# FNet and gMLP on one core: third buffer for h2's rows, and waiting steps moved behind the splits that PE needs

## The chip, the core and the metric

The kernel runs on 1 core of one Trainium2 chip. The metric is the time of one execution on the device in microseconds (us): 943.65, the median of 3 runs (942.11 to 944.61). Only the order of the work and one buffer are changed, so a result is a difference of two such times.

## The reference

All tensors are float32. x is 2048 x 512, and c gives six rows (sa, ca, ga, sb, cb, gb) by a product with w_mod.

```python
h = _layernorm(x) * (1 + ca) + sa
a = h @ dft_hid_re.T;  b = h @ dft_hid_im.T
y = dft_seq_re @ a - dft_seq_im @ b          # 2048 x 2048 matrices
x = x + ga * y
h = _layernorm(x) * (1 + cb) + sb
z = gelu(h @ w_in)                           # 512 x 1792
z1, z2 = z[:, :896], layernorm(z[:, 896:])
x = x + gb * ((z1 * (w_sp @ z2 + b_sp)) @ w_out)   # w_sp 2048 x 2048
```

(The original writes these as einsums with a batch of 1; the equations are the same.)

## The kernel before

**Splits.** TensorE (PE) multiplies in fp32r. Every float32 operand is split into a high part (ScalarE, ACT: a copy into fp32r, line 604 for the pairs `ph`, 267 for `ah`) and a low part (VectorE, DVE: source minus high part, line 608 `pl`, 274 `al`). Each product is three matmuls (`matmul3`, lines 97 to 99): high by high, low by high, high by low. So PE needs, for each chunk of work, a `pl` or `al` that DVE has just made; each of these sits in a ring of three buffers (`ph`, `pl` and `al`; four for `ah`). Most chunks are twelve matmuls of 512 columns.

**Stages in order of time.** The *a* stage and three *t* stages make the sequence transform in four quarters t = 0 to 3. In a t stage there are 14 chunks of kind s and 16 of kind k. The k chunks use source blocks that are transposed on DVE (`tp`, line 539) straight out of a load buffer. The s chunks use sums and differences of blocks (one Strassen-like level): `f`, transposed at line 539, combined at 573 (`sum_f`). Results lie in PSUM banks `gs..c11`, `u`, `v`, `c22`; when a product form is done, banks are copied or subtracted (lines 682 and 688, t = 1 only, into `gs_u` and `um`), and at the end of a quarter `out_k` (line 723) adds `um` and stores to `g_d` through GpSimd's (POOL's) DMA queue. The *y* stage multiplies with the hidden-dimension matrices (`hr`, read as `hraw` and transposed at line 188), one block of 128 rows in 24 matmuls. For each row block m: `seed_y` (853) copies x into the PSUM bank `yp`, `split_g` (92, 93) makes `gh`/`gl`, PE accumulates, `post_y` (865) copies `x2` out and takes statistics (DVE 105, 107; POOL 109, 110, 117), `norm_y` (121) makes `h2` on ACT in a ring of two buffers, `post_h` (875 to 877) scales it on DVE and stores it to `h2_d` from POOL's queue. The *z1* stage multiplies `h2` (loaded again, transposed as `t`, line 238, or `hz`) with the first half of w_in, with seven product forms; banks `z1p`, `z1g`, the latter copied from the former at 988. Then *z2* (second half, banks `z2p`), the *w* stage with w_sp (`gw`), and the last product (`op`).

**Combinations of w_sp** are made on the way. For twelve of sixteen units in the z1 and z2 stages, four before: `load_s` reads three pieces (tile `sj`, lines 1056, 1058, SP's queue), `sum_s` adds and subtracts on DVE (1063, 1064, 1067) and stores to `s_d` (1070, POOL's queue). `sj` has two buffers in z1 and z2; in the t stages it uses the two buffers `stage`, which also hold the source blocks. A load into a buffer waits until the stores out of it have landed.

**What sets the order.** Nothing is scheduled by a tool: each engine runs its instructions in the order in which the program issues them. PE's chunks are numbered n, and `atd(n, f, ...)` puts a step f behind chunk n (n + 0.5: behind the low split that is made ahead there). `D1` = 32 is the first t chunk, `DT` = 30 chunks a quarter, `Y0` = 122 the first of 32 y chunks, `YE` = 154 the first z1 chunk. `CHUNKS[t]` is the order in which source blocks are loaded; a block's buffer is handed to the load two blocks on when its last transpose is issued (`block_done`). SP, ACT, DVE and POOL wait in order: whatever waits holds the rest of its queue.

Of the kernel before, what the change touches and what calls it, by code (L numbers as in the profile page):

```python
# [8 lines left out]
F32 = mybir.dt.float32  # L9
F32R = mybir.dt.float32r  # L10
AF = mybir.ActivationFunctionType
ALU = mybir.AluOpType

P = 128
# [5 lines left out]
def fnet_gmlp_kernel(  # L20
# [32 lines left out]
    nc = tc.nc  # L53
    S, D = x.shape[1:]
# [3 lines left out]
    NQ = S // Q  # L58
# [66 lines left out]
    def at(n, f, *a):  # L125
        fill.setdefault(n, []).append((f, a))
# [10 lines left out]
    def quad_s(t, role):  # L137
# [1 line left out]

    src = [quad((cr, ci)[j], 0, g) for g in range(NQ) for j in range(2)]  # L140
    CHUNKS = {1: (("k", 1, 0), ("k", 1, 1), ("s", 2, 21), ("s", 2, 11), ("k", 1, 2), ("k", 1, 3), ("s", 2, 22)),
              2: (("s", 3, 21), ("s", 3, 11), ("k", 2, 0), ("k", 2, 1), ("k", 2, 2), ("s", 3, 22), ("k", 2, 3)),
              3: (("k", 3, 0), ("k", 3, 1), ("k", 3, 2), ("k", 3, 3))}
    order_b = {}
    for t in range(1, NQ):
# [5 lines left out]
    N2 = 4 * len(src)  # L151
# [71 lines left out]
    def turn_two(n):  # L223

        if n >= NE:
            return
        b, k = divmod(n - SKIP if n >= N3 else n, 4)
        st = stage[b]
        t = blocks.tile([P, 2, Q], F32, tag="t", bufs=2, name=f"t{n}")
        T[n], T[n + 1] = t[:, 0, :], t[:, 1, :]  # L230
        if n >= N4:
            nc.vector.transpose(t.rearrange("p r (b i) -> p r b i", i=32), st[:, :, :, 16 * k:16 * k + 32])  # L232
        elif n >= N3:
            for m in range(2):
                nc.vector.transpose(T[n + m].rearrange("p (k a i) -> p a k i", k=4, i=32),
                                    st[:, :, 32 * (k + m):32 * (k + m) + 32].rearrange("p (a k) i -> p a k i", k=4))
        else:
            nc.vector.transpose(t.rearrange("p k (b i) -> p k b i", i=32),
                                st[:, :, 32 * k:32 * k + 64].rearrange("p b (k i) -> p k b i", k=2))
        if n == N2:  # L240
            RAW[0, 1] = RAW[0, 6] = t
        elif n == N2 + 2:
            RAW[0, 2] = RAW[0, 3] = t
        if k == 2:
            stage.pop(b)
            load(b + 2)

    RAW = {}

# [40 lines left out]
    fpool, yp, hrp = [], [], []  # L290
# [366 lines left out]
    def set_of(t, role):  # L657

        return {"c11": 0, "u": 2 if t == 3 else 4, "v": 4 if t == 3 else 2, "c22": 6}[role]

    def mm_s(t, i):
        p, m = ORD[i // 2], i % 2
        acc = {1: "c11", 2: "c11", 5: "v", 3: "v", 6: "u", 7: "u", 4: "u"}[p]
        fresh = p in (1, 5) and t > 1
        if m == 0 and fresh:
            for f in range(2):
                C[acc, f] = bank(set_of(t, acc) + f, f"gs{t}_{acc}_{f}")
        if t not in UM and p == 5:
            UM[t] = outs.tile([P, 4, D], F32, tag="um", bufs=1, name=f"um{t}")
        u = at_unit["s", t, i]  # L670
        ph, pl = PH.pop(u), PL.pop(u)
        for c_ in range(2):
            for f in range(2):
                matmul3(C[acc, f], *form_v(p, 2 * m + c_, f), ph[:, c_, :], pl[:, c_, :],
                        fresh and m == 0 and c_ == 0, m == 1 and c_ == 1, not fresh)
        if m == 0:
            return
        for f in range(2):
            if p == 1:
                C["u", f] = bank(set_of(t, "u") + f, f"gs{t}_u_{f}")  # L680
                if t == 1:
                    nc.vector.tensor_tensor(C["u", f], C["c11", f], UM[t][:, f, :], op=ALU.subtract)
                else:
                    nc.scalar.activation(C["u", f], C["c11", f], AF.Copy)
            elif p == 5:
                um = UM[t][:, 2 + f, :]
                if t == 1:
                    nc.vector.tensor_tensor(um, C["v", f], um, op=ALU.subtract)
                else:
                    nc.scalar.activation(um, C["v", f], AF.Copy)  # L690
            elif p == 6:
                nc.scalar.activation(UM[t][:, f, :], C["u", f], AF.Copy)
            elif p == 7:
                C["c22", f] = bank(set_of(t, "c22") + f, f"gs{t}_c22_{f}")
                nc.scalar.activation(C["c22", f], C["u", f], AF.Copy)
# [171 lines left out]
        NRM["y", m] = norm([X["2", m]], "y")  # L867

    def norm_y(m):
        LN["y", m] = yp[0].tile([P, D], F32, tag="h2", bufs=2, name=f"h2_{m}")  # L870
        apply(LN["y", m], X.pop(("2", m)), NRM.pop(("y", m)))

    def post_h(m):
# [422 lines left out]
    lo_one(2)  # L1296
    lo_h(1)

    n_now = [0]

    def atd(n, f, *a):

        at(("d", n) if n < YE else N2 + int(n - YE), f, *a)
# [44 lines left out]
    for t in range(1, NQ):  # L1348
        o = D1 + DT * (t - 1)
        d = 8 if t == 1 else 0  # L1350
        for m in range(2):
            atd(o + d + 0.5 + m, sum_f, t, 6, m)
            atd(o + d + 6 + m, sum_f, t, 3, m)
        for j in range(2):
            atd(o + ((22, 29) if t == 1 else (21, 29))[j], *((out_last, j) if t == NQ - 1 else (out_k, t, j)))
        if t < NQ - 1:
            atd(o + (11 if t == 1 else 3.5), load_sb, t + 1, 12)
            for role, n, m in (((21, 13, 14), (11, 15.5, 16.5), (12, 17.5, 18.5), (22, 24, 25)) if t == 1 else
                               ((21, 3, 5), (11, 7.5, 8.5), (12, 9.5, 10.5), (22, 21, 23))):
                atd(o + n, turn_s, t + 1, role, 0)  # L1360
                atd(o + m, turn_s, t + 1, role, 1)
            for p, n, m in (((5, 26, 26.5), (7, 27, 28)) if t == 1 else ((5, 24, 26), (7, 27, 28))):
                atd(o + n, sum_f, t + 1, p, 0)
                atd(o + m, sum_f, t + 1, p, 1)

# [13 lines left out]
            atd(n + k + 1, sum_column, j, k)  # L1379
    atd(83, scale_columns)  # L1380
    for j, l, ns, m, k, plus_one in ((2, 37, (40, 41, 42), 44, 6, False), (4, 51, (56, 57, 58), 60, 3, True),
                                     (3, 58.5, (63, 64, 65), 66, 7, False), (5, 77.5, (82, 83, 85), 87, 0, False)):
        atd(l, load_mod, j)
        atd(ns[0], sum_mod, j, [0, 1])
        atd(ns[1], sum_mod, j, [2, 3])
        atd(ns[2], split_mod, j)
        atd(m, spread_mod, j, k, plus_one)
    early = ((44.5, 53), (85.5, 89), (86.5, 91), (112.5, 115.5))
    early += tuple((YE + n, YE + m) for n, m in ((14, 17), (15, 19), (19, 27), (21, 28), (28, 31), (29, 33), (32, 35),
                                                 (34, 37), (36, 39), (38, 41), (39, 42), (41, 44)))  # L1390
    for (n, m), u in zip(early, [(r, g, b) for g in range(2) for b in range(4) for r in range(2)]):
        atd(n, load_s, *u)
        atd(m, sum_s, *u, True)
        atd(m + (m < YE + 23), sum_s, *u, False)
    atd(93, load, order_b["k", 3, 0])
    atd(96.5, load, order_b["k", 3, 1])
    hrs = ctx.enter_context(ExitStack())
    o = D1 + 2 * DT

# [5 lines left out]
        tf.close()  # L1405
        yp.append(p2.enter_context(pool("ypool", "right")))

    for n, *todo in ((-6, (load_ht, 0)), (-3, (turn_ht, 0, 0)), (-2, (turn_ht, 0, 1)), (-1, (turn_ht, 0, 2)), (0, (turn_ht, 0, 3)), (8, (scale_w0, 0)),
                     (9, (load_ht, 1), (weigh_ht, 0, 0), (weigh_ht, 0, 1)), (10, (weigh_ht, 0, 2), (weigh_ht, 0, 3), (load_w0, 0)),
                     (12, (fold_ht, 0, 0), (fold_ht, 0, 1)), (13, (fold_ht, 0, 2), (fold_ht, 0, 3)),  # L1410
                     (14, (open_hr,), (split_acc, 0), (turn_ht, 1, 0), (scale_w0, 1), (read_row, 2, hrp)),
# [48 lines left out]
    for n, *todo in ((0, (load_gelu,)), (2, (change_w,)), (4, (load_wi, 0, 2)), (7, (hi_w, 1)), (8, (lo_w, 1)), (9, (hi_w, 2)), (10, (lo_w, 2)), (11, (sum_w, 5)),  # L1460
                     (12, (sum_w, 6)), (13, (hi_w, 6)), (14, (lo_w, 6)), (15, (sum_w, 7), (load, N2 // 4)), (17, (sum_w, 4)),
                     (18, (hi_w, 7)), (19, (lo_w, 7), (turn_two, N2)), (20, (prep_hi, N2), (hi_w, 4)),
                     (21, (prep_lo, N2), (load, N2 // 4 + 1), (lo_w, 4)), (22, (prep_hi, N2 + 1)), (23, (prep_lo, N2 + 1)),
                     (26, (turn_z, 1)), (27, (sum_z, 0)), (28, (turn_two, N2 + 2), (prep_hi, N2 + 2)), (29, (prep_lo, N2 + 2)),
                     (30, (prep_hi, N2 + 3))):
        for f, *a in todo:
            atd(Y0 + n, f, *a)

# [4 lines left out]
    n = 0  # L1473
    for u, (kind, t, i) in enumerate(units):
        for m in range(1 if kind == "s" else 2):
            ahead = kind == "s" or m and u > 2
            if ahead:
                pipeline(u)
            if kind == "a":
                mm_a(n)  # L1480
            elif kind == "s":
                mm_s(t, i)
            else:
                mm_k(t, i, m)
            n_now[0] = n
            run(("d", n))
            if ahead:
                lo_unit(u + 2)
            run(("d", n + 0.5))
            n += 1  # L1490
# [141 lines left out]
```

## Time and profile before

| | |
|---|---|
| median of 3 runs | 943.65 us (942.11 to 944.61) |
| the profiled execution | 942.02 us, of which 940.3 us from the first instruction to the last |
| granted TensorE clock, mean | 0.998 |
| PE busy | 927.7 us (99%) |
| DVE busy | 746.6 us (79%) |
| ACT busy | 433.4 us (46%) |
| HBM | 135.01 MB read, 43.00 MB written |

A row of a timeline gives start, length, engine, line, operation, the tile written and the tiles read (their numbers left out), shapes, count, and in brackets the idle time before it and what ended it. A matmul's shown length (0.39) is longer than its distance to the next, since matmuls are pipelined. The waits list counts only gaps of over 150 ns.

### The profile page before, as it was taken

The numbers are of one execution on the slowest core, as the hardware profiler recorded it, in microseconds if no ns is written. First come the engines' busy times: TensorE is split into PE (matmuls) and PEld (weight loads), VectorE is DVE, ScalarE is ACT, GpSimd is POOL, SyncE is SP. The second block draws the span as 40 slices with busy tenths as digits, with TensorE's granted clock in tenths as the row PEclk, the third lists the DMA queues.
The fourth block names the chain that finished last, engine by engine and source line by source line (L and its number), as shares of the span: only waits on it lengthen the run. The fifth ranks groups of instructions, "written<-read, shape, count | busy, mean of one in ns | idle before, by whom it ended". The sixth has DMA issues, their size and how long they took to land.

```text
span 940.3 us, 12142 instructions
## 1 busy us (share of the span) xinstructions
PE 927.7 (99%) x4088; PEld 768.2 (82%) x4088; DVE 746.6 (79%) x1016; ACT 433.4 (46%) x686; POOL 158.6 (17%) x312
## 2 busy tenths in 40 slices
PE   9999999999999999999999999999999999999998
PEld 6788878888778888887878999888888888888886
DVE  7879789899788884778768667998789688885972
ACT  3585344354354353555765456553544444331221
POOL 1331001100110004544323444301000000000000
PEclk9999999999999999999999999999999999999999
DMA  9998949798685626795799876997569746743641
GB/s 203 217 210 187 224 98 235 182 171 192 173 232 105 180 83 195 227 267 166 212 328 273 242 236 213 262 259 207 124 151 261 201 111 157 185 112 113 198 160 57
DMA packets 269375, 178.83 MB, mean 190 GB/s; under 512 B 135168, under 2 KB 233728, under 8 KB 269184
## 3 DMA queue, kind: packets, MB, share of 16 engines
q1 hardware_dynamic: 253744, 133.99, 59.3%
q0 software_dynamic: 12576, 41.44, 11.7%
q10 hardware_dynamic: 2992, 2.62, 1.2%
q8 instruction: 32, 0.52, 0.2%
q14 instruction: 31, 0.25, 0.1%
HBM read 135.01 MB, written 43.00 MB: 189 GB/s over the span
## 4 chain that ended last, share of the span: by engine, by line
PE 71%; issue 11%; DVE 7%; DMA 5%; POOL 2%; SPq 1%; ACT 1%; DVEq 0%; ACTq 0%; POOLq 0%
PE gw L98 9%; PE gw L99 9%; PE gw L97 9%; PE op L99 3%; PE op L98 3%; PE op L97 3%; PE gp L98 2%; PE gp L99 2%; PE gp L97 2%; PE z2p L97 2%; PE z2p L99 2%; PE z2p L98 2%; PE gs_c L98 2%; PE gs_c L99 2%; PE gs_c L97 2%
## 5 line engine op out<-in xcount | busy, mean ns | idle before, releaser
L98 PE MATMUL gw<-al,bh 128*128 128x512 f32 x400 | 155.7, 389 | 0.1
L99 PE MATMUL gw<-ah,bl 128*128 128x512 f32 x400 | 155.6, 389 | 0.0
L97 PE MATMUL gw<-ah,bh 128*128 128x512 f32 x400 | 155.6, 389 | 0.0
L274 DVE TENSOR_TENSOR al<-t,ah 128x512 fp32r<-128x512 f32 x136 | 92.5, 686 | 61.9 <-PE gw L98 35.3
L267 ACT ACTIVATE ah<-t 128x512 fp32r<-128x512 f32 x136 | 84.9, 626 | 101.6 <-PE gw L99 56.0
L98 PEld LDWEIGHTS gw<-al,bh 128*128 128x128 f32 x400 | 75.1, 188 | 16.2 <-DVE al L274 0.5
L99 PEld LDWEIGHTS gw<-ah,bl 128*128 128x128 f32 x400 | 75.1, 188 | 15.5
L97 PEld LDWEIGHTS gw<-ah,bh 128*128 128x128 f32 x400 | 75.1, 188 | 15.5
L232 DVE STREAM_TRANSPOSE t<-stage 128x1024 f32<-128x1024 f32 x56 | 69.4, 1239 | 0.1
L604 ACT ACTIVATE ph<-f 128x1024 fp32r<-128x1024 f32 x42 | 44.4, 1058 | 40.4 <-PE gs_c L99 12.4
L1106 ACT ACTIVATE bh<-z 128x512 fp32r<-128x512 f32 (+1 forms) x56 | 32.8, 586 | 62.4 <-PE gw L98 60.6
L608 DVE TENSOR_TENSOR pl<-f,ph 128x1024 fp32r<-128x1024 f32 x42 | 50.7, 1214 | 11.6 <-ACT ph L604 11.5
L98 PE MATMUL gs_c<-pl,hh 128*128 128x512 f32 x144 | 56.3, 391 | 1.3 <-DVE pl L608 1.1
L99 PE MATMUL gs_c<-ph,hl 128*128 128x512 f32 x144 | 56.1, 389 | 0.0
L97 PE MATMUL gs_c<-ph,hh 128*128 128x512 f32 x144 | 56.1, 389 | 0.0
L604 ACT ACTIVATE ph<-tp 128x1024 fp32r<-128x1024 f32 x35 | 36.9, 1055 | 39.3 <-PE gs_v L99 15.9
L539 DVE STREAM_TRANSPOSE tp<-stage 128x1024 f32<-128x1024 f32 x36 | 44.4, 1232 | 4.4 <-DMA stage<-in_A_dft_seq_im_dram 4.1
L1070 POOL DMA_DIRECT2D s_d<-sj x48 | 26.6, 554 | 122.3 <-DVE sj L1063 105.0
L608 DVE TENSOR_TENSOR pl<-tp,ph 128x1024 fp32r<-128x1024 f32 x35 | 42.3, 1210 | 5.6 <-ACT ph L604 5.6
L98 PE MATMUL z2p<-wil,ah 128*128 128x448 f32 x128 | 46.7, 365 | 0.0
L97 PE MATMUL z2p<-wih,ah 128*128 128x448 f32 x128 | 46.7, 365 | 0.0
L99 PE MATMUL z2p<-wih,al 128*128 128x448 f32 x128 | 46.7, 365 | 0.0
(288 smaller groups left out, 2235.9 us busy)
## 6 DMA issues: line engine op xcount, KB each, us to landing
stage<-s_d SPq DMA_DIRECT2D x128, 128.0 KB, 2.9
stage<-in_A_dft_seq_re_dram SPq DMA_DIRECT2D x52, 256.0 KB, 6.6
s_d<-sj POOLq DMA_DIRECT2D x48, 256.0 KB, 5.2
stage<-in_B_w_sp_dram SPq DMA_DIRECT2D x96, 128.0 KB, 3.1
stage<-in_A_dft_seq_im_dram SPq DMA_DIRECT2D x44, 256.0 KB, 5.3
sj<-in_B_w_sp_dram SPq DMA_DIRECT2D x16, 512.0 KB, 6.7
stage<-h_d SPq DMA_DIRECT2D x32, 256.0 KB, 7.0
gr<-g_d SPq DMA_DIRECT2D x12, 512.0 KB, 5.7
```

The source lines that it names most:

```text
L97: nc.tensor.matmul(acc, ah, bh, start=first, stop=False, skip_group_check=go_on)
L98: nc.tensor.matmul(acc, ah, bl, start=False, stop=False, skip_group_check=go_on)
L99: nc.tensor.matmul(acc, al, bh, start=False, stop=last, skip_group_check=go_on)
L232: nc.vector.transpose(t.rearrange("p r (b i) -> p r b i", i=32), st[:, :, :, 16 * k:16 * k + 32])
L267: nc.scalar.activation(AH[n], source(n), AF.Copy)
L274: nc.vector.tensor_tensor(AL[n], source(n), AH[n].bitcast(F32), op=ALU.subtract)
L539: nc.vector.transpose(dst.rearrange("p k (b i) -> p k b i", i=32), st[:, :, 64 * m:64 * m + 64].rearrange("p b (k i) -> p k b i", k=2))
L604: nc.scalar.activation(pair_of(PH, u, "ph"), source_unit(u), AF.Copy)
L608: nc.vector.tensor_tensor(pair_of(PL, u, "pl"), source_unit(u), PH[u].bitcast(F32), op=ALU.subtract)
L1070: nc.gpsimd.dma_start(s_d[m, r, g][b * P:(b + 1) * P, :], a)
L1106: nc.scalar.activation(BH[p, k][:, :w], b_of(p, k), AF.Copy)
```

## The change

- `h2` gets three buffers in place of two.
- A new helper `later` puts a step half a chunk on, behind the low split made there. The subtractions of t = 1 (lines 682, 688) go through it. Some other steps get half a chunk more in the tables: `out_k` and `out_last`, first sums of w_sp units.
- In t = 2 the block ("k", 2, 3) is loaded ahead of ("s", 3, 22), and the turns and sums that need the latter come two or three chunks later.
- hr's real part is loaded 1.5 chunks earlier, and its four turns come 4.5 to 5.5 chunks later, spread. The split of `wm5` comes one chunk earlier. The first two blocks of t = 3 are loaded 2 and 1.5 chunks earlier.
- z1's second turn, `turn_two(N2 + 2)`, and its splits (`t130`, `ah130`, `ah131`, `al130`) come 4 to 5 chunks earlier, within y; the load that this turn used to issue keeps its place as a step of its own.
- From the first w_sp unit of z1 on, the twelve pairs (load, sum) get new places: the first two sums come 3 chunks later with the same loads, so six and seven chunks behind them.

```diff
-              2: (("s", 3, 21), ("s", 3, 11), ("k", 2, 0), ("k", 2, 1), ("k", 2, 2), ("s", 3, 22), ("k", 2, 3)),
+              2: (("s", 3, 21), ("s", 3, 11), ("k", 2, 0), ("k", 2, 1), ("k", 2, 2), ("k", 2, 3), ("s", 3, 22)),
...
         if k == 2:
             stage.pop(b)
-            load(b + 2)
+            if n != N2 + 2:
+                load(b + 2)
...
+    def later(f, *a):
+        at(("d", n_now[0] + 0.5), f, *a)
...
-                    nc.vector.tensor_tensor(C["u", f], C["c11", f], UM[t][:, f, :], op=ALU.subtract)
+                    later(nc.vector.tensor_tensor, C["u", f], C["c11", f], UM[t][:, f, :], ALU.subtract)
...
-        LN["y", m] = yp[0].tile([P, D], F32, tag="h2", bufs=2, name=f"h2_{m}")
+        LN["y", m] = yp[0].tile([P, D], F32, tag="h2", bufs=3, name=f"h2_{m}")
...
-            atd(o + d + 0.5 + m, sum_f, t, 6, m)
+            atd(o + (7.5 if t == 1 else 0.5) + m, sum_f, t, 6, m)
...
-    early += tuple((YE + n, YE + m) for n, m in ((14, 17), (15, 19), (19, 27), (21, 28), (28, 31), (29, 33), (32, 35),
-                                                 (34, 37), (36, 39), (38, 41), (39, 42), (41, 44)))
+    early += tuple((YE + n, YE + m) for n, m in ((14, 20), (15, 22), (22, 28), (24, 29), (29, 32), (30, 33), (32, 35),
+                                                 (33, 37), (35, 39), (37, 41), (39, 42), (41, 44)))
...
-    for n, *todo in ((-6, (load_ht, 0)), (-3, (turn_ht, 0, 0)), (-2, (turn_ht, 0, 1)), (-1, (turn_ht, 0, 2)), (0, (turn_ht, 0, 3)), (8, (scale_w0, 0)),
+    for n, *todo in ((-7.5, (load_ht, 0)), (1.5, (turn_ht, 0, 0)), (2.5, (turn_ht, 0, 1)), (4.5, (turn_ht, 0, 2)), (5.5, (turn_ht, 0, 3)), (8, (scale_w0, 0)),
```

The order of PE's instructions is the same. DVE around the last k chunks of t = 2, before (`pl57` and `pl58` are low splits that PE needs; `stage21` is the block that was loaded last, `f3_22` a block for t = 3):

```order
L608 TENSOR_TENSOR pl56_2118<-tp56_2057,ph56_2093 128x1024
L317 TENSOR_SCALAR wm5_2035<-wm5_2035,sc_136 128x512
L319 SCALAR_TENSOR_TENSOR wm5_2035<-wm5_2035,sc_136 128x512
L539 STREAM_TRANSPOSE tp58_2137<-stage21_2097 128x1024
L723 TENSOR_TENSOR um2_1727<-gs2_v_0_1725,um2_1727 128x512
L723 TENSOR_TENSOR um2_1727<-gs2_v_1_1726,um2_1727 128x512
L539 STREAM_TRANSPOSE f3_22_2161<-stage20_2015 128x1024
L348 TENSOR_SCALAR col1_141<-col1_141 128x4
L349 TENSOR_SCALAR col2_142<-col1_141 128x4
L319 SCALAR_TENSOR_TENSOR wm5_2035<-wm5_2035,sc_136 128x512 x2
L608 TENSOR_TENSOR pl57_2167<-tp57_2095,ph57_2135 128x1024
```

and now:

```order
L609 TENSOR_TENSOR pl56_2118<-tp56_2057,ph56_2093 128x1024
L318 TENSOR_SCALAR wm5_2035<-wm5_2035,sc_136 128x512
L320 SCALAR_TENSOR_TENSOR wm5_2035<-wm5_2035,sc_136 128x512
L540 STREAM_TRANSPOSE tp58_2137<-stage20_2015 128x1024
L349 TENSOR_SCALAR col1_141<-col1_141 128x4
L350 TENSOR_SCALAR col2_142<-col1_141 128x4
L320 SCALAR_TENSOR_TENSOR wm5_2035<-wm5_2035,sc_136 128x512 x2
L609 TENSOR_TENSOR pl57_2155<-tp57_2095,ph57_2135 128x1024
L729 TENSOR_TENSOR um2_1727<-gs2_v_0_1725,um2_1727 128x512
L729 TENSOR_TENSOR um2_1727<-gs2_v_1_1726,um2_1727 128x512
```

`um2` and the turn of `f3_22` moved from ahead of `pl57` to behind it, and `tp58` reads the block that is loaded first. On DVE in z1, before (`al148` to `al150` are low splits that PE needs, `sj002` the w_sp unit):

```order
L1063 TENSOR_TENSOR sj002_4169<-sj002_4169 128x512
L1064 TENSOR_TENSOR sj002_4169<-sj002_4169 128x512
L901 TENSOR_TENSOR wil1_0_4245<-wraw1_0_3995,wih1_4243 128x896
L274 TENSOR_TENSOR al148_4271<-hz3_4126,ah148_4237 128x512
L1067 TENSOR_TENSOR sj002_4169<-sj002_4169 128x512
```

and now:

```order
L907 TENSOR_TENSOR wil1_0_4241<-wraw1_0_3995,wih1_4239 128x896
L275 TENSOR_TENSOR al148_4267<-hz3_4126,ah148_4237 128x512
L907 TENSOR_TENSOR wil1_1_4272<-wraw1_0_3995,wih1_4239 128x896
L275 TENSOR_TENSOR al149_4286<-hz3_4126,ah149_4269 128x512
L944 TENSOR_TENSOR hz2_4024<-hz2_4024 128x1024
L275 TENSOR_TENSOR al150_4309<-hz3_4126,ah150_4288 128x512
L1069 TENSOR_TENSOR sj002_4169<-sj002_4169 128x512
L1070 TENSOR_TENSOR sj002_4169<-sj002_4169 128x512
L275 TENSOR_TENSOR al151_4327<-hz3_4126,ah151_4311 128x512
```

Three low splits now stand ahead of the first sum of `sj002`. On ACT late in y, before (`yp` rows are seeds, `x2` rows the copies out of the bank):

```order
L865 ACTIVATE x2_9_3734<-yp9_3643 128x512
L853 ACTIVATE yp11_3746<-xr11_3647 128x512
L267 ACTIVATE ah130_3755<-t130_3748 128x512
L121 ACTIVATE h2_8_3757<-x2_8_3680,nmry_3690,rsy_3687 128x512
L865 ACTIVATE x2_10_3788<-yp10_3692 128x512
```

and now, two row blocks earlier (the line numbers are those of the changed kernel, up to six higher):

```order
L859 ACTIVATE yp9_3645<-xr9_3533 128x512
L268 ACTIVATE ah130_3647<-t130_3614 128x512
L121 ACTIVATE h2_6_3649<-x2_6_3576,nmry_3586,rsy_3583 128x512
L92 ACTIVATE gh10_3665<-gr10_3562 128x1024
L871 ACTIVATE x2_8_3686<-yp8_3588 128x512
L859 ACTIVATE yp10_3698<-xr10_3594 128x512
```

`ah130` moved from between the seed of `yp11` and `h2_8` to between the seed of `yp9` and `h2_6`.

More of the change, by code (lines that the diff above doesn't have):

```diff
@@ L659, in set_of @@
         return {"c11": 0, "u": 2 if t == 3 else 4, "v": 4 if t == 3 else 2, "c22": 6}[role]
+    n_now = [0]
+    def later(f, *a):
+        at(("d", n_now[0] + 0.5), f, *a)
     def mm_s(t, i):
@@ L687, in mm_s @@
                 if t == 1:
-                    nc.vector.tensor_tensor(um, C["v", f], um, op=ALU.subtract)
+                    later(nc.vector.tensor_tensor, um, C["v", f], um, ALU.subtract)
                 else:
@@ L1297, in fnet_gmlp_kernel @@
     lo_h(1)
-    n_now = [0]
     def atd(n, f, *a):
@@ L1351, in fnet_gmlp_kernel @@
         for m in range(2):
-            atd(o + d + 0.5 + m, sum_f, t, 6, m)
+            atd(o + (7.5 if t == 1 else 0.5) + m, sum_f, t, 6, m)
             atd(o + d + 6 + m, sum_f, t, 3, m)
         for j in range(2):
-            atd(o + ((22, 29) if t == 1 else (21, 29))[j], *((out_last, j) if t == NQ - 1 else (out_k, t, j)))
+            atd(o + ((22.5, 29.5) if t == 1 else (21.5, 29) if t == 3 else (21.5, 29.5))[j], *((out_last, j) if t == NQ - 1 else (out_k, t, j)))
         if t < NQ - 1:
@@ L1358, in fnet_gmlp_kernel @@
             for role, n, m in (((21, 13, 14), (11, 15.5, 16.5), (12, 17.5, 18.5), (22, 24, 25)) if t == 1 else
-                               ((21, 3, 5), (11, 7.5, 8.5), (12, 9.5, 10.5), (22, 21, 23))):
+                               ((21, 3, 5), (11, 7.5, 8.5), (12, 9.5, 10.5), (22, 24, 25))):
                 atd(o + n, turn_s, t + 1, role, 0)
                 atd(o + m, turn_s, t + 1, role, 1)
-            for p, n, m in (((5, 26, 26.5), (7, 27, 28)) if t == 1 else ((5, 24, 26), (7, 27, 28))):
+            for p, n, m in (((5, 26, 26.5), (7, 27, 28)) if t == 1 else ((5, 26, 26.5), (7, 27, 28))):
                 atd(o + n, sum_f, t + 1, p, 0)
@@ L1381, in fnet_gmlp_kernel @@
     for j, l, ns, m, k, plus_one in ((2, 37, (40, 41, 42), 44, 6, False), (4, 51, (56, 57, 58), 60, 3, True),
-                                     (3, 58.5, (63, 64, 65), 66, 7, False), (5, 77.5, (82, 83, 85), 87, 0, False)):
+                                     (3, 58.5, (63, 64, 65), 66, 7, False), (5, 77.5, (82, 83, 84), 87, 0, False)):
         atd(l, load_mod, j)
@@ L1387, in fnet_gmlp_kernel @@
         atd(m, spread_mod, j, k, plus_one)
-    early = ((44.5, 53), (85.5, 89), (86.5, 91), (112.5, 115.5))
-    early += tuple((YE + n, YE + m) for n, m in ((14, 17), (15, 19), (19, 27), (21, 28), (28, 31), (29, 33), (32, 35),
-                                                 (34, 37), (36, 39), (38, 41), (39, 42), (41, 44)))
+    early = ((44.5, 53.5), (85.5, 88.5), (87.5, 91.5), (112.5, 115.5))
+    early += tuple((YE + n, YE + m) for n, m in ((14, 20), (15, 22), (22, 28), (24, 29), (29, 32), (30, 33), (32, 35),
+                                                 (33, 37), (35, 39), (37, 41), (39, 42), (41, 44)))
     for (n, m), u in zip(early, [(r, g, b) for g in range(2) for b in range(4) for r in range(2)]):
@@ L1394, in fnet_gmlp_kernel @@
         atd(m + (m < YE + 23), sum_s, *u, False)
-    atd(93, load, order_b["k", 3, 0])
-    atd(96.5, load, order_b["k", 3, 1])
+    atd(91, load, order_b["k", 3, 0])
+    atd(95, load, order_b["k", 3, 1])
     hrs = ctx.enter_context(ExitStack())
@@ L1462, in fnet_gmlp_kernel @@
                      (18, (hi_w, 7)), (19, (lo_w, 7), (turn_two, N2)), (20, (prep_hi, N2), (hi_w, 4)),
-                     (21, (prep_lo, N2), (load, N2 // 4 + 1), (lo_w, 4)), (22, (prep_hi, N2 + 1)), (23, (prep_lo, N2 + 1)),
-                     (26, (turn_z, 1)), (27, (sum_z, 0)), (28, (turn_two, N2 + 2), (prep_hi, N2 + 2)), (29, (prep_lo, N2 + 2)),
-                     (30, (prep_hi, N2 + 3))):
+                     (21, (prep_lo, N2), (load, N2 // 4 + 1), (lo_w, 4)), (22, (prep_hi, N2 + 1)), (23, (prep_lo, N2 + 1), (turn_two, N2 + 2)),
+                     (24, (prep_hi, N2 + 2)), (25, (prep_lo, N2 + 2)), (26, (turn_z, 1)), (27, (sum_z, 0)), (28, (prep_hi, N2 + 3)),
+                     (29, (load, N2 // 4 + 2))):
         for f, *a in todo:
@@ L1475, in fnet_gmlp_kernel @@
         for m in range(1 if kind == "s" else 2):
-            ahead = kind == "s" or m and u > 2
+            ahead, n_now[0] = kind == "s" or m and u > 2, n
             if ahead:
@@ L1484, in fnet_gmlp_kernel @@
                 mm_k(t, i, m)
-            n_now[0] = n
             run(("d", n))
```

## The prediction

> **What bounds the kernel now.** I read the page first, then the waits of TensorE (PE), then the timelines of PE, VectorE (DVE) and ScalarE (ACT) around each wait.
>
> ```profile
> PE 927.7 (99%) x4088; PEld 768.2 (82%) x4088; DVE 746.6 (79%) x1016; ACT 433.4 (46%) x686; POOL 158.6 (17%) x312
> L608 DVE TENSOR_TENSOR pl<-f,ph 128x1024 fp32r<-128x1024 f32 x42 | 50.7, 1214 | 11.6 <-ACT ph L604 11.5
> ```
>
> The matmuls are the bound, and the change leaves their number and order alone. So only the time in which PE stands still can be won. The waits of PE name it: engine, line, what it waited for, then us in total, times, longest.
>
> ```profile
> PE z1g L98 <- DVE al L274: 2.2, 1, 2.2
> PE busyp L355 <- DVE busy L298: 1.4, 1, 1.4
> PE yp L97 <- ACT yp L853: 1.2, 3, 0.6
> PE gs_c L98 <- DVE pl L608: 1.1, 1, 1.1
> PE gp L98 <- DVE pl L608: 1.1, 1, 1.1
> PE gs_u L98 <- DVE pl L608: 0.7, 1, 0.7
> PE z1p L97 <- ACT z1g L988: 0.6, 1, 0.6
> PE gs_v L98 <- DVE pl L608: 0.4, 1, 0.4
> ```
>
> busyp and gp lie in the first 40 us, which the change doesn't touch. The other six rows are eight stalls, 6.2 us idle. A stall costs more than its idle time, as the timeline of PE at the gs_u wait shows (start, length, line):
>
> ```profile
> 245.22 0.39 PE L97 MATMUL gs_c<-ph,hh 128*128 128x512 f32 x1
> ...
> 245.90 0.39 PE L97 MATMUL gs_u<-ph,hh 128*128 128x512 f32 x1
> 246.97 0.50 PE L98 MATMUL gs_u<-pl,hh 128*128 128x512 f32 x1 [0.69 <-DVE pl L608]
> 247.31 0.39 PE L99 MATMUL gs_u<-ph,hl 128*128 128x512 f32 x1
> ```
>
> Undisturbed, three matmuls take 245.22 to 245.90, 0.227 us each; a chunk of twelve takes 2.72. Here two steps took 1.41 in place of 0.45: 0.96 lost for 0.69 idle. I take idle plus 0.27 for a short stall. The long one, in z1, is worse; its PE timeline, then the stretches around it with the granted clock (PEclk, third value from the end):
>
> ```profile
> 488.41 0.39 PE L97 MATMUL z1g<-ah,w 128*128 128x512 f32 x1
> 490.97 0.73 PE L98 MATMUL z1g<-al,w 128*128 128x512 f32 x1 [2.17 <-DVE al L274]
> ...
> 494.48 0.40 PE L97 MATMUL z1g<-ah,w 128*128 128x512 f32 x1
> ```
> ```profile
> 484.00:488.00 4.00, 4.00 (x20) 3.30 (x19) 0.11 (x1) 3.18 (x6) 0.00 (x0) 1.00 1.08 330
> 491.00:494.40 3.40, 3.40 (x8) 2.75 (x9) 3.37 (x6) 0.00 (x0) 2.19 (x5) 0.51 0.95 374
> ```
>
> After 2.17 us idle the clock was granted at 0.51 for 3.4 us: 8 matmuls in that stretch. From 488.41 to 494.48 are nine steps (490.97, then seven at half speed, then 494.48), 6.07 us in place of 2.04. This stall costs 4.0. [...]
>
> **The change, place by place.** DVE and ACT work their queues in order, so a step that waits holds all behind it. Timeline of DVE at the four t-stage places:
>
> ```profile
> 122.89 1.38 DVE L682 TENSOR_TENSOR gs_u<-gs_c,um 128x512 f32<-128x512 f32 x2 [0.82 <-PE gs_c L99]
> 124.18 1.53 DVE L319 SCALAR_TENSOR_TENSOR wm<-wm,sc 128x512 f32<-128x512 f32 x2
> 125.63 1.22 DVE L608 TENSOR_TENSOR pl<-f,ph 128x1024 fp32r<-128x1024 f32 x1
> ...
> 240.52 1.25 DVE L539 STREAM_TRANSPOSE tp<-stage 128x1024 f32<-128x1024 f32 x1 [3.38 <-DMA stage<-in_A_dft_seq_im_dram]
> 241.69 1.25 DVE L723 TENSOR_TENSOR um<-gs_v,um 128x512 f32<-128x512 f32 x2
> ...
> 245.70 1.22 DVE L608 TENSOR_TENSOR pl<-tp,ph 128x1024 fp32r<-128x1024 f32 x1
> ...
> 259.51 0.71 DVE L188 STREAM_TRANSPOSE hr<-hraw 128x512 f32<-128x512 f32 x1 [2.61 <-DMA hraw<-in_A_dft_hid_re_dram]
> 260.15 1.18 DVE L608 TENSOR_TENSOR pl<-f,ph 128x1024 fp32r<-128x1024 f32 x1
> ...
> 266.73 1.18 DVE L608 TENSOR_TENSOR pl<-f,ph 128x1024 fp32r<-128x1024 f32 x1
> ```
>
> *Subtractions later (t=1).* The gs_u pair (1.38, plus 0.82 waiting for PE) moves behind the pl that PE waited for: that pl ends 2.2 earlier, the stall was 0.4 idle. The moved pair is next asked for by the u chunks, one chunk (2.72) after that pl is, and follows it at once, 1.38 long: covered. The sum_f step put ahead costs one 1.22, the like of which goes from behind: nothing. What is put behind pl35 and pl39 feeds stores, what is put behind pl79 isn't asked for before the y stage, chunks later: nothing. Won: 0.4 + 0.27.
>
> *Block order of t=2.* DVE stood 3.38 us for a block and had um next, with pl57 behind both. Now the block that pl57's neighbours need is loaded first, and um, f and the other block come after. From the start of that idle time (237.14): turn 1.25, col and wm an estimated 1.5 (from um's end at 242.94 to pl57's start at 245.70, less the one turn between), pl 1.22, so pl57 ends near 241.1, against 246.1 when PE asks. 5 us of room. Won: 0.7 + 0.27.
>
> *hr's load earlier, its turns later.* Ahead of pl61 go 2.61 of waiting and three turns of 0.7, 4.7 in all, against 1.1 idle; the turns now stand behind pl63, pl64, pl66 and pl67, one each, where 0.7 a chunk of 2.72 fits. What is new: on SP's queue hr's four DMAs pass two w_sp loads, so sj100 lands later, and pl60 and pl61 stand behind its sum. The old run shows no wait for sj100, so I bound it from nothing to the 2.61 that the transfer last in line cost; both are under the 4.7 removed less 1.1, 3.6. I take nothing. The two loads of t=3's blocks, put one or two chunks earlier, wait for the sj stores anyway. Won: 1.1 + 0.27.
>
> *y stage.* ACT's waits there, and its timeline at the last two stalls:
>
> ```profile
> ACT h L121 <- DMA h_d<-h: 19.4, 7, 5.4
> ```
> ```profile
> 423.26 0.81 ACT L121 ACTIVATE h<-x,nmry,rsy 128x512 f32<-128x512 f32 x1 [5.39 <-DMA h_d<-h]
> ...
> 425.40 0.59 ACT L853 ACTIVATE yp<-xr 128x512 f32<-128x512 f32 x1
> ...
> 439.03 0.63 ACT L267 ACTIVATE ah<-t 128x512 fp32r<-128x512 f32 x1 [9.27 <-DVE t L238]
> ...
> 442.75 0.59 ACT L988 ACTIVATE z1g<-z1p 128x512 f32<-128x512 f32 x1
> ```
>
> With two buffers an h2 row waits for the store of the row two before; the seed (yp) for PE is two instructions behind it. A third buffer asks for a store one row block older, 24 matmuls or 5.4 us, as long as the longest wait: all seven go. The z1p stall came from ah130 (9.27 us idle for its turn on DVE), with h2, x2 and z1g behind it. ah130 and its turn now stand five chunks, some 13 us, earlier. They cost ACT 0.63 and DVE 1.25 plus 0.7 for al130 ahead of gh11 and gl11; the ACT side fits in the 5.39 freed, on DVE I take it as covered by the same, with under 1 us to spare. The load of h2_d1 stays where it was on SP. Won: 1.2 + 3 x 0.27, and 0.6 + 0.27.
>
> *w_sp sums behind their loads.* DVE in z1:
>
> ```profile
> 480.30 0.69 DVE L274 TENSOR_TENSOR al<-hz,ah 128x512 fp32r<-128x512 f32 x1 [0.43 <-PE z1p L98]
> 487.89 0.69 DVE L1063 TENSOR_TENSOR sj<-sj 128x512 f32<-128x512 f32 x1 [6.90 <-DMA sj<-in_B_w_sp_dram]
> ...
> 490.23 0.69 DVE L274 TENSOR_TENSOR al<-hz,ah 128x512 fp32r<-128x512 f32 x1
> ```
>
> DVE was idle for 6.90 us for the load, and al148 stood three steps behind. Now al148, al149, al150 come first, so al148 is ready as soon as PE's buffers allow. The next that can be late is al151, behind two sums; PE asks for it two chunks of nine matmuls and one of twelve later, 6.8 us after 488.41. If the load lands when it did relative to PE, al151 can be done by 490.0 (three steps of 0.7) and has 5 us. Won: 4.0, the clock included.
>
> Sum: idle 0.4 + 0.7 + 1.1 + 1.2 + 0.6 = 4.0; seven short stalls at 0.27 make 1.9; with 4.0 for z1, 9.9. The profiled execution took 942.02, so it would take 932.1; the median of the three before is 943.65, 1.6 higher, and I forecast from it: 933.7.
>
> **Rivals.** *The y stage stays late.* x2's statistics pass through POOL before ACT can make h2. POOL's middle step (min, median, max in ns) in that stage:
>
> ```profile
> L110 POOL TENSOR_TENSOR rsy<-mvy,mhalf x16: 560/567/1599, 364.7 to 447.6; 128x1 f32<-128x1 f32 x16
> ```
>
> At three steps of up to 1.6 the chain is 4.8 in place of 1.7; if DVE, now packed closer, makes them all long, h2 comes 3 us later, and the seeds behind it have lost most of the room. Against it: the long ones are few, the median is near the minimum. Price: the y part, 2.9; time 936.6. [...]
>
> *The w_sp load doesn't move with PE.* PE comes 5.9 earlier to z1; if the load still lands at 487.89, al151 ends at 490.0 against 489.3 due: 0.7 + 0.27 lost, 934.7. The loads before it are released by PE's own progress, so I hold this the less likely.
>
> *The change doesn't do what it says at the end of t=2:* sj100, behind hr's DMAs, lands over 3.6 us late and the gs_u or gs_c stall stays: up to 2.3 lost, 936.0.
>
> *Slower.* The later w_sp units come through two buffers: a load waits for the store of the unit two before. Their sums come later too, so each store and each next load does, and DVE waits in z2 with al behind it. It already did once; columns as above:
>
> ```profile
> 527.02 0.69 DVE L1063 TENSOR_TENSOR sj<-sj 128x512 f32<-128x512 f32 x1 [1.29 <-DMA sj<-in_B_w_sp_dram]
> ...
> 539.24 1.27 DVE L274 TENSOR_TENSOR al<-t,ah 128x512 fp32r<-128x512 f32 x2
> ```
>
> If the 8.2 us (three chunks) by which the first sums move came back as waiting at each later pair, PE would stall past 2.2 us, at 4.0 each with the clock. Three of them, one for each further group of z2, are 12.0, over the 9.9 won: 945.7 (before: 943.65). It decides from a wait of about 4 us, an estimate: al at 539.24 stands 12 us behind the wait of 1.29, and PE's list has no wait for it. Against it: the later pairs' sums move by one or two chunks, some by none, and each load's room grows with its sum.
>
> **How the numbers follow.** Chances: forecast 0.60; y stays late 0.15; load not moving 0.10; t=3 0.05; several of these and one new stall with the half clock (933.7 + 2.9 + 4.0 and some, about 941) 0.05; slower 0.05. Under 0.3%, 2.8 us, is about what a measurement can't tell from no change. The first four are faster, 0.90; the fifth is the same; the last slower. The range takes the first four: from 931.5 (below the sum against the profiled execution, for stalls too short for the list) to 937.5 (y and the load together).
>
> **What would show it.** Right: PE's waits list keeps gp and busyp and loses z1g, yp, gs_c, gs_u, gs_v, z1p; PEclk is 1.00 through z1; ACT no longer waits for h_d. Wrong: a PE wait of over 1 us anywhere after 40 us, above all on al in z1 or z2, or on yp; DVE waiting for sj ahead of an al that PE lacks; the end near 938 with the list empty, which would say that idle time isn't the price.

## The result, and the profile after

The changed kernel takes 932.72 us (median of 5 runs, 931.02 to 933.23); the kernel before, 942.34 beside it (5 runs, 941.05 to 944.61). The ratio is 0.989, 95% interval 0.9871 to 0.9908: 9.6 us won, where 9.9 was forecast. The profiled execution took 933.23, its span 931.5.

The waits of PE, after, whole (engine, line, what it waited for, us in total, times, longest):

```profile
PE gp L636 <- DVE ph L1279: 1.5, 1, 1.5
PE busyp L356 <- DVE busy L299: 1.4, 1, 1.4
PE gp L98 <- DVE pl L609: 1.3, 1, 1.3
PE gw L98 <- DVE al L275: 0.8, 2, 0.6
```

All six rows that the forecast meant to remove are gone, and the granted clock is 1.00 from 450 to 490 us, through z1g's place. The first three rows lie in the first 40 us. The last is new: it lies at the start of the w stage. How much each stretch is worth is read from the same matmul in both timelines of PE. Before, then after (start, length, line; in brackets the idle time before it):

```profile
36.43 0.50 PE L98 MATMUL gp<-pl,hh 128*128 128x512 f32 x1 [1.12 <-DVE pl L608]
...
599.37 0.50 PE L98 MATMUL gw<-al,bh 128*128 128x512 f32 x1
```

```profile
37.27 0.50 PE L98 MATMUL gp<-pl,hh 128*128 128x512 f32 x1 [1.29 <-DVE pl L609]
...
484.66 0.39 PE L97 MATMUL z1g<-ah,w 128*128 128x512 f32 x1
...
590.58 0.50 PE L98 MATMUL gw<-al,bh 128*128 128x512 f32 x1 [0.23 <-DVE al L275]
```

At 36 us this execution was 0.84 behind the one before. The matmul that stood at 494.48 now stands at 484.66, 9.82 ahead: 10.66 won in between. At the w stage's third split PE is 8.79 ahead: 1.03 given back, and so it stays to the end. So the pair of profiles shows 8.8 us, the medians 9.6.

The y stage: ACT's waits for h, after.

```profile
ACT h L121 <- POOL nmry L117: 11.2, 5, 7.3
ACT h L121 <- DMA h_d<-h: 1.4, 1, 1.4
```

19.4 us of waiting for h_d in seven places became 1.4 in one. ACT now waits for POOL instead, with no stall of PE behind it. POOL's middle step still has its long ones (558/564/1526 ns), so they alone didn't make y late.

DVE at the end of t = 2 and in z1, after:

```profile
239.95 1.22 DVE L609 TENSOR_TENSOR pl<-tp,ph 128x1024 fp32r<-128x1024 f32 x1
241.08 1.28 DVE L729 TENSOR_TENSOR um<-gs_v,um 128x512 f32<-128x512 f32 x2
...
477.24 0.68 DVE L275 TENSOR_TENSOR al<-hz,ah 128x512 fp32r<-128x512 f32 x1
...
482.65 0.69 DVE L275 TENSOR_TENSOR al<-hz,ah 128x512 fp32r<-128x512 f32 x1 [0.29 <-issue]
483.26 0.69 DVE L1069 TENSOR_TENSOR sj<-sj 128x512 f32<-128x512 f32 x1
483.98 0.69 DVE L1070 TENSOR_TENSOR sj<-sj 128x512 f32<-128x512 f32 x1
484.70 0.69 DVE L275 TENSOR_TENSOR al<-hz,ah 128x512 fp32r<-128x512 f32 x1
```

pl57 ends at 241.17 (forecast: near 241.1). In z1 the sums follow three splits and find their load landed: no wait stands before them. al151, at 484.70, ends 4.3 us before the matmul that takes it (489.64); 5 were forecast.

The new wait, at the z2 to w edge, is DVE's:

```profile
578.39 0.69 DVE L275 TENSOR_TENSOR al<-t,ah 128x512 fp32r<-128x512 f32 x1 [3.93 <-PE z2p L99]
579.00 1.24 DVE L232 STREAM_TRANSPOSE t<-stage 128x1024 f32<-128x1024 f32 x1
581.21 0.69 DVE L1069 TENSOR_TENSOR sj<-sj 128x512 f32<-128x512 f32 x1 [0.97 <-DMA sj<-in_B_w_sp_dram]
...
586.57 0.67 DVE L275 TENSOR_TENSOR al<-t,ah 128x512 fp32r<-128x512 f32 x1
```

From 578.39 to 586.57 DVE is idle only for the 0.97 in which it waits for the last w_sp unit (sj113), and PE waits for that last split. Before, the sums found their load landed there; PE lost 0.4. The load's own queue shows why it is late. POOL's store out of the buffer, then SP's load into it, before and after:

```profile
576.32 1.71 POOL L1070 DMA_DIRECT2D s_d<-sj  x3
581.74 0.33 SPq L1056 DMA_DIRECT2D sj<-in_B_w_sp_dram  x1
```

```profile
566.45 1.70 POOL L1076 DMA_DIRECT2D s_d<-sj  x3
574.16 0.35 SPq L1062 DMA_DIRECT2D sj<-in_B_w_sp_dram  x1
```

The stores are issued 9.9 us earlier, as PE comes 9.8 earlier; the load that waits for them is issued 7.6 earlier only. From the last store's issue (its row's end) to the load went 3.7 us before, 6.0 now. The load didn't keep step with PE. Why these stores took longer to land isn't settled, and it changes from execution to execution: in two of the experiments below the same stretch took 7.3 (changed_again, the same kernel) and 4.5 (last_sum_later).

### The profile page after: what moved, and what is told of

Read it like the earlier page. It is cut to its first block, busy times and chain, and to the rows that moved or that the text cites. A ratio compares the mean times of both kernels' runs of the same rounds, so it can differ in the third digit from the quotient of the medians.

```text
span 931.5 us, 12149 instructions
## 1 busy us (share of the span) xinstructions
PE 922.7 (99%) x4088; PEld 767.7 (82%) x4088; DVE 747.2 (80%) x1016; ACT 432.6 (46%) x686; POOL 156.3 (17%) x312
## 4 chain that ended last, share of the span: by engine, by line
PE 90%; DMA 4%; DVE 3%; SPq 1%; issue 1%; ACT 0%; DVEq 0%; ACTq 0%
PE gw L98 9%; PE gw L99 9%; PE gw L97 9%; PE gs_c L98 4%; PE gs_c L99 4%; PE gs_c L97 3%; PE yp L99 3%; PE yp L98 3%; PE yp L97 3%; PE op L99 3%; PE op L98 3%; PE op L97 3%; PE gs_u L97 3%; PE gs_u L99 3%; PE gs_u L98 3%; PE gp L98 2%
```

## The experiments

"Lost" below is always the distance from one matmul to the next, less the usual 0.227, summed over a stall and the few steps behind it.

**The edge, and a version that cures it.** Three kernels on one chip, beside the kernel before (944.65, 11 runs, 940.71 to 946.84).

The first is the changed kernel unaltered.

> The changed kernel as it is, beside the next two on the same chip. Theory (its gain is the idle time and the restarts of PE's eight late stalls, all gone): again 9 to 10 us under the kernel before, about 0.990 of it. PE's trace between 40 and 586 us keeps one stall, gs_c near 218 us (0.4 lost). The w stage's first splits: the trace of the changed kernel lost 1.43 us there (0.98 and 0.34 behind one another, 0.36 in the kernel before). If that is this kernel's own (DVE held 0.97 us for the last w_sp unit's load), it shows again, 1 to 1.5 us; if it was a chance of that one execution, 0.3 to 0.4.

931.08 (6 runs, 930.57 to 933.41), ratio 0.9866 (0.9842 to 0.9889). That is 13.6 us under the kernel before, by the interval 10.5 to 14.9: more than the 9 to 10 expected. Seven of the eleven executions of the kernel before were slower here than the 942.02 of the profile from which the sum was made. DVE and PE at the edge:

```profile
581.37 0.69 DVE L1069 TENSOR_TENSOR sj<-sj 128x512 f32<-128x512 f32 x1 [2.66 <-DMA sj<-in_B_w_sp_dram]
```

```profile
PE gw L98 <- DVE al L275: 2.6, 2, 2.3
```

A longer wait than 0.97, and a longer stall: 3.1 lost, over the 1.5 expected. The stall at the edge shows in both profiles of this kernel, and its size changes from execution to execution. The second kernel moves the last unit's sums:

```diff
-                (33, 37), (35, 39), (37, 41), (39, 42), (41, 44)))
+                (33, 37), (35, 39), (37, 41), (39, 42), (41, 47)))
```

> The changed kernel with the last w_sp unit's two sums behind chunk 47 in place of 44, so behind the first three low splits of the w stage. Theory (DVE is what PE waits for at the z2 to w edge: 0.97 us of waiting for the load and 2.1 us of sums stand ahead of al175): the two gw stalls go, 1.4 us under the changed kernel run beside it, about 931.3. Rival (the six statistics of z2's rows, not the sums, set the edge, and the freed time is filled by them): the stall falls to no less than the 0.36 of the kernel before, 1.0 us. Rival (the stores of this unit, later now, hold the load of the later w rows): a new wait in w, no gain.

930.54 (5 runs, 930.42 to 930.92), ratio 0.9861 (0.9837 to 0.9884). PE's list keeps only the first 40 us:

```profile
PE busyp L356 <- DVE busy L299: 1.4, 1, 1.4
PE gp L98 <- DVE pl L609: 0.5, 1, 0.5
```

The edge costs nothing now, not even the 0.4 of before; so it was the sums and their wait, not the statistics. The median moved by 0.5, less than the 1.4 expected, but the runs above 931 are gone. The third kernel has this and one more edit:

```diff
-    for j, l, n in ((1, 66.5, 73), (0, 73, 78)):
+    for j, l, n in ((1, 66.5, 73.5), (0, 73, 78)):
```

> As the last one, and wt's four turns and products of the first column group (two engines, DVE and ACT) half a chunk later, behind the low split there. Theory: the gs_c stall near 218 us (pl52 is ready 0.05 us after PE wants it, behind a turn of 0.67 and a product of 0.69) goes too, 0.42 more: 1.8 us under the changed kernel, about 930.9. Rival: the moved pair makes pl53 or pl54 late instead (room 1.9 and 3.7 us, the pair takes 1.36), and the 0.42 stays.

930.12 (5 runs, 929.77 to 930.24), ratio 0.9855 (0.9832 to 0.9878): all its runs lie under all those of the changed kernel on that chip. No stall at 218 us is left, and the median is 0.42 under the second kernel's, as expected; it is 1.0 under the changed kernel's, where 1.8 was expected. This is the best version found.

**One part at a time.** Six kernels have one part alone on the kernel before.

```diff
-        ... tag="h2", bufs=2 ...
+        ... tag="h2", bufs=3 ...
```

> The kernel before with three buffers for h2's rows and nothing else. Theory: ACT waits no more for h_d, the three yp stalls (0.54, 0.62 and 0.95 lost) go, 2.1 in all; z1p's 0.92 and z1g's stay. Rival (the y stage is late through x2's statistics on POOL, and the buffer only hides it): at least one yp stall of 0.5 or more stays, with ACT waiting for POOL ahead of the seed.

940.75 in one run. PE's list has no wait between 280 and 485 us: the three yp stalls went, and z1p's with them, which wasn't expected.

The next has the turn and its splits moved, with h2 in two buffers (the edits to `turn_two`'s load and to the table of y steps in the diff above).

> The kernel before with z1's second turn and its splits earlier in y, and nothing else. Theory: z1p's stall (0.92 lost) goes; the three yp stalls stay, since h2 has two buffers still. Rival (the moved split of 0.63 on ACT and the turn of 1.25 on DVE, without the third buffer to hide them, come on top): the yp stalls grow by about what is moved, 0.6 or more, and the edit alone gains nothing.

942.75 in one run. PE's waits in y and at z1p:

```profile
PE yp L97 <- ACT yp L854: 0.9, 1, 0.9
PE yp L99 <- DVE gl L93: 0.4, 1, 0.4
```

z1p's stall went here too; the y stage lost 2.1 us (0.31, 1.14 and a new one at 433 on gl, 0.69), as much as its three yp stalls did before (2.1). So each of two edits removes z1p's stall by itself. To see whether the changed kernel needs both, the turn was put back in it (with the last w_sp sums behind chunk 47, as above):

```diff
-  (23, (prep_lo, N2 + 1), (turn_two, N2 + 2)), (24, (prep_hi, N2 + 2)), ...
+  (23, (prep_lo, N2 + 1)), ... (28, (turn_two, N2 + 2), (prep_hi, N2 + 2)), ...
```

> The changed kernel with the last w_sp sums behind chunk 47, and z1's second turn and its splits back in their old places. With the third h2 buffer alone the z1p stall was gone too. Theory now (that stall came from ACT's waits for h_d, not from the turn's place): no yp, z1p or z1g stall here, the same span as with the turn moved (929.1). Rival (as the prediction had it: the turn's place makes it): a z1p stall of 0.9 near 434 us, seen now that PE comes earlier.

930.59 in one run, span 928.8 against 929.1 with the turn moved (last_sum_later). ACT in that kernel:

```profile
429.56 0.63 ACT L267 ACTIVATE ah<-t 128x512 fp32r<-128x512 f32 x1 [8.01 <-DVE t L238]
...
434.69 0.58 ACT L993 ACTIVATE z1g<-z1p 128x512 f32<-128x512 f32 x1 [0.95 <-PE z1p L99]
```

ACT waits 8.01 us for the turn, as it did 9.27 before, and still is early: z1g's copy waits for PE, not PE for it. So the turn's old place alone doesn't stall PE; moving it isn't needed once h2 has three buffers. The kernel before shows how the two belong together. ACT's wait of 5.39 for h_d makes gh late, DVE waits 2.29 for it ahead of gl at 425.06, and from there DVE works without a gap to the end of the turn at 439.0, with ACT's ah130 and z1g's copy behind it. With three buffers the turn starts at 435.04 in place of 437.79; with the turn moved, the copy behind it starts at 442.80, in time for the matmul at 444.00. Either takes off enough: the stall was 0.9.

> The kernel before with the new places of the twelve w_sp pairs and nothing else. Theory (the edits add up, each taking its own stall): the z1g stall near 488 us goes, 4.06 us in the profiled execution before (2.3 where the clock isn't halved); all stalls ahead of it stay. At the z2 to w edge the last unit's load comes late as in the changed kernel, 1.4 to 4.0 lost against 0.36 before, so net 0.3 to 3 us under the kernel before. Rival (that edge is late only because PE comes 10 us earlier to it, while DMA traffic stays where it was): in this kernel PE comes 4 us earlier only, and the edge costs under 1 us.

939.87 (10 runs, 936.67 to 942.55) against 943.18 (13 runs); ratio 0.9962 (0.9945 to 0.998). The z1g stall is gone; the edge lost 1.1, which lies between the two bounds set. 3.3 us won (by the interval 1.9 to 5.2), where 0.3 to 3 was expected.

> The kernel before with t = 1's subtractions half a chunk later and the sum_f pair that goes with them, and nothing else. Theory: the gs_v stall near 126 us (0.83 lost in all three executions of that code seen, 0.81 to 0.83 spacing gaps) goes and nothing comes in its place in t = 1; all later stalls stay. Rival (the sum_f step put ahead makes a split late instead): a stall of 0.5 or more between 100 and 180 us.

942.89 in one run: no stall between 40 and 216 us. The edge, with the old places of the w_sp pairs and PE no earlier than before, lost 1.7 in this execution, DVE waiting 1.25 for sj. So this stall can come without the change.

> The kernel before with the two last blocks of t = 2 in the other order and the turns and sums that need them later, and nothing else. Theory: the gs_u stall near 246 us (0.97 to 1.24 lost) goes; the gs_c stall near 266 us stays, since it comes from hr's load and turns. Rival (the t = 2 end is one queue, and what is put behind pl57 and pl58 makes pl60 and pl61 later): the gs_c stall grows by a turn or two, 1.2 or more over the 1.4 to 2.7 seen.

940.4 in one run: the gs_u stall is gone, gs_c's is 1.2, not larger.

> The kernel before with hr's load 1.5 chunks earlier, its turns later, the w_sp pairs and block loads that go with them, and nothing else. Theory: the gs_c stall near 266 us goes (1.44, 2.33, 2.47 and 4.47 lost in four executions of the old code, so its worth is 1.4 to 4.5 and not the 1.4 of one execution); gs_u near 246 stays. Rival (the load of hr ahead of w_sp's makes pl60 and pl61 wait for their sums): a stall of 0.5 or more at 255 to 270 us, DVE waiting for sj.

939.62 in one run: no gs_c stall at 266; DVE waits 1.81 for sj ahead of the sums, and PE doesn't notice. How the stall hangs on hr's load is seen where that edit is absent, in DVE's first turn and PE's list. z1_sums_alone, then h2_three_alone:

```profile
260.20 0.71 DVE L188 STREAM_TRANSPOSE hr<-hraw 128x512 f32<-128x512 f32 x1 [3.63 <-DMA hraw<-in_A_dft_hid_re_dram]
```

```profile
PE gs_c L98 <- DVE pl L608: 2.2, 1, 2.2
```

```profile
261.20 0.71 DVE L188 STREAM_TRANSPOSE hr<-hraw 128x512 f32<-128x512 f32 x1 [3.90 <-DMA hraw<-in_A_dft_hid_re_dram]
```

```profile
PE gs_c L98 <- DVE pl L608: 2.6, 1, 2.6
```

With the kernel before (wait 2.61, stall 1.1) they give one line, on which the other three executions without that edit lie too: PE's stall is the load's wait less 1.3 to 1.5. One execution's stall is a sample. What each place lost in all profiled executions in which its own edit was absent, and in the changed kernel (for the edge, the ladder below among them):

| place | profile of before | others | after |
|---|---|---|---|
| gs_v, 126 us | 0.83 | 0.83 to 0.90 (5) | 0 |
| gs_u, 246 | 0.97 | 1.03 to 1.24 (5) | 0 |
| gs_c, 266 | 1.4 | 1.2, 2.4, 2.6, 3.9, 4.5 | 0 |
| yp and z1p, 380 to 442 | 3.0 | 1.7 to 3.8 (4) | 0 |
| z1g, 488 | 4.1 | 2.6, 3.7, 4.1, 4.3, 4.4 | 0 |
| the w edge, 598 | 0.4 | 0.4, 0.4, 0.4, 0.4, 1.7 | 1.4, 3.1, 4.0 |

That fits the spread of the kernel before, 940.7 to 946.8, and of the best version, half a microsecond; only the profiled executions show their stalls, so for the others it is argued.

**What a stall costs.** Needless statistics steps on DVE in the w stage make PE stand still. The two kernels that have them take 971.28 and 953.32, in one run each.

```diff
+    for k, c in ((22, 8), (34, 9), (46, 10), (58, 11), (70, 12), (82, 13), (94, 14)):
+        at(N4 + k, delay, k, c)      # c times bn_stats of 512 elements
```

> The changed kernel with 8, 9, 10, 11, 12, 13 and 14 needless statistics steps (512 elements, an estimated 0.6 us each by the 0.57 that the 448 wide one takes) on DVE at seven places of the w stage, 12 chunks apart, to make PE stand still for lengths that rise from about 0 to 3.5 us. The output is the reference's. Theory: a stall costs its idle time plus 0.27 up to a length between 1.5 us (the gp stall near 35 us, no drop) and 2.17 us (z1's, a drop); above that the clock is granted at about 0.5 for 3.4 us and the stall costs 1.7 more. [...]

Its edge stall, and two of the made ones, on PE (idle time in brackets), with the stretches behind them (third value from the end: granted clock):

```profile
587.90 0.50 PE L98 MATMUL gw<-al,bh 128*128 128x512 f32 x1 [2.14 <-DVE al L275]
...
651.94 0.50 PE L98 MATMUL gw<-al,bh 128*128 128x512 f32 x1 [2.28 <-DVE al L275]
...
749.99 0.50 PE L98 MATMUL gw<-al,bh 128*128 128x512 f32 x1 [1.10 <-DVE al L275]
```

```profile
589.20:592.40 3.20, 3.20 (x9) 2.52 (x8) 3.10 (x7) 2.65 (x4) 2.35 (x6) 0.50 0.38 151
652.00:655.40 3.40, 3.40 (x15) 2.80 (x16) 3.11 (x5) 0.17 (x1) 0.14 (x1) 1.00 0.26 77
```

2.14 idle halves the clock (0.50), and 2.28 doesn't (1.00): length alone isn't it. The short stall of 1.10 lost 1.39, idle plus 0.29, so the 0.27 holds. So ten more stalls were made, with the same number of steps each and with the last sums later as above, to see which of them draw the slow clock:

```diff
+    for k, c in ((20, 8), (29, 8), (38, 8), (47, 8), (56, 8), (65, 8), (74, 8), (83, 8), (92, 8), (101, 8)):
```

> The changed kernel with the last w_sp sums behind chunk 47, and 8 needless statistics steps on DVE at each of ten places of the w stage, 9 chunks apart, for ten stalls of about the same length, 1.5 to 2.5 us idle. The output is the reference's. [...]

Three of its stalls, and the clock behind each:

```profile
643.12 0.50 PE L98 MATMUL gw<-al,bh 128*128 128x512 f32 x1 [2.98 <-DVE al L275]
...
689.30 0.59 PE L98 MATMUL gw<-al,bh 128*128 128x512 f32 x1 [1.89 <-DVE al L275]
...
715.40 0.50 PE L98 MATMUL gw<-al,bh 128*128 128x512 f32 x1 [1.65 <-DVE al L275]
```

```profile
643.40:646.80 3.40, 3.40 (x16) 2.79 (x16) 3.40 (x6) 2.41 (x5) 0.08 (x1) 1.00 0.41 162
689.70:692.60 2.90, 2.90 (x8) 2.30 (x7) 2.39 (x5) 0.74 (x2) 0.00 (x0) 0.50 0.03 6
715.60:719.00 3.40, 3.40 (x16) 2.78 (x16) 3.37 (x6) 0.67 (x2) 0.16 (x1) 1.00 0.57 199
```

The longest, 2.98, draws nothing (clock 1.00); one of 1.89 does (0.50), the only one in that run; the 1.65 doesn't (1.00). The slow stretch at the ladder's edge and the one here last 3.4 us, by the starts of their first and last slow matmuls: 589.16 and 592.53, 689.30 and 692.68. Two kernels above bear out that length alone isn't it: behind z1_sums_alone's gs_c stall, 2.17 idle like z1g's in the profile of before, the clock is 1.00 (269.0 to 272.4), where z1g's drew 0.51; behind h2_three_alone's, 2.58 idle, it is 0.53 (269.7 to 273.0). The ladder's theory, a drop above some length between 1.5 and 2.17, falls. What decides beside the length isn't shown.

## Why the prediction was right, and where not

**The sum.** 10.66 us were won between 36 and 485 us of the timeline after, against 9.9 in the sum. By place, forecast and lost in the profile of before: gs_v 0.67 and 0.83, gs_u 0.97 and 0.97, gs_c 1.4 and 1.4, yp 2.0 and 2.1, z1p 0.9 and 0.9, z1g 4.0 and 4.1, and 0.2 at 342 us that was too short for the list. "Idle plus 0.27 for a short stall" held. The sum was made from one execution; by the table, gs_c's term could have come out 3 us higher in another, and z1g's 1.5 lower. So each stall was rightly found, but that 9.6 came so near to 9.9 is in part luck: the same two kernels lay 13.6 apart when they were run again, and 8.8 in the pair of profiles.

**z1p: the right size, half the cause.** "The z1p stall came from ah130 (9.27 us idle for its turn on DVE)": moving the turn does remove it, but three buffers alone remove it too, and the turn in its old place doesn't bring it back. The stall took both, a late y and the turn behind it. The prediction counted an edit for it that the third buffer made needless.

**The clock.** The half clock behind z1g was read rightly from its row, and the loss of 4.0 with it. The row shows that 2.17 can halve the clock, not that it always does: 2.28 didn't in the ladder, and 2.17 didn't in z1_sums_alone. z1g lost 2.6 in an execution where the stall came in two pieces.

**The edge: the step that failed.** "The later pairs' sums move by one or two chunks, some by none, and each load's room grows with its sum." The last pair's sum and load weren't moved at all, but PE came 9.8 us earlier and that load, which waits for a store, was issued only 7.6 earlier. One of the prediction's signs of being wrong came with it: "DVE waiting for sj ahead of an al that PE lacks". It is the slower rival's chain (store, load, sum, split) at one place in place of three, at the end of z2 and not in its middle, with 1.0 more than before in the profiled execution and 2.7 more in another. All three executions with the new places and these sums unmoved, where PE comes its full 9 us earlier, lost 1.4 or more there; of the six with the old places, one did.

**The other rivals.** Y didn't stay late. z1's load moved with PE: no wait stands before its sums. At the end of t = 2 DVE does wait for sj, 1.58 us before the first sum, inside the room of 3.6 that the prediction left it. The gs_c stall near 218 us (0.4), in both kernels, was under the list's bound and wasn't named; best_try shows that half a chunk cures it.

## What to carry to other kernels

Where one engine is the bound, sum its stalls and their restarts, but take each from several executions: a stall that hangs on a transfer is a sample. When a gain upstream brings the bound engine forward, look at every later load that waits for a store: it may not come forward with it. Undo a part of a change before you believe what it was for, and try each part alone as well; here either of two edits removed one stall, and one buffer did what both were made for.

## What the runs showed of the hardware

- Behind stalls of PE of 1.89 (repeated_stall), 2.14 (ladder), 2.17 (the kernel before) and 2.58 us (h2_three_alone) the TensorE clock was granted at 0.50 to 0.53 in the 2.9 to 3.4 us that were read behind them; behind stalls of 1.10 and 2.28 (ladder), 1.65 and 2.98 (repeated_stall) and 2.17 (z1_sums_alone) it stayed at 1.00. The stall of 2.98 cost 3.3 us, the one of 1.89 3.8.
- From the issue of the last of the same three stores of 256 KB to that of the load that waits for them, it took 3.7 us in the kernel before and 6.0 in the changed one, with the DMA engines 62% and 64% busy; 7.3 in changed_again (69%) and 4.5 in last_sum_later (61%); the cause stays open.
